# Attention with a K/V cache: the loads at the start are reordered, and the first block's Q projection is interleaved with attention

## The chip, the cores and the metric

The kernel runs on one core of a Trainium2 chip. The metric is device time in microseconds (us); lower is better. A ratio is the mean time of one kernel's fast runs over that of the other's fast runs in the same rounds, so it is not quite the ratio of the medians that are quoted beside it. The engines: PE does the matmuls (PEld loads their weights), ACT the exponentials, DVE the other elementwise work, POOL is the one that gpsimd calls address; SP only issues loads. A DMA queue is named after the engine that issues into it. The DMA share adds up the packets' own times over 16 DMA engines, so it can pass 1.

## The reference

```python
B, Sq, D = 8, 208, 1024
H, Sk, Dh = 32, 1024, 128
# x: (B,Sq,D); k_cache, v_cache: (B,H,Sk,Dh); wq: (D,H*Dh); wo: (H*Dh,D); all bfloat16

def reference(x, k_cache, v_cache, wq, wo):
    q = transpose((x @ wq).reshape(B, Sq, H, Dh), 0, 2, 1, 3)
    scores = einsum("bhqd,bhkd->bhqk", q, k_cache) * (Dh ** -0.5)
    p = softmax(scores, axis=-1)
    o = einsum("bhqk,bhkd->bhqd", p, v_cache)
    return transpose(o, 0, 2, 1, 3).reshape(B, Sq, H * Dh) @ wo
```

## The kernel before

The work is cut into 32 blocks (4 groups of 8 heads, times 8 batches) of 8 units; a unit is one head of one batch. Units are pipelined: PE makes the scores of the next unit while ACT takes the exponential, and PE multiplies by V one half unit later. Two lists of small pieces fill PE's gaps: one piece of Q projection for a later block, and one piece of output projection, per unit. K and x come in by DMA transpose on the SP queue, V by plain copy on the SP queue, and the weights by plain copy on the gpsimd queue.

```python
    xT = const.tile([128, DT, NTOK], BF16, name="xT_all")
    nc.sync.dma_start_transpose(out=xT[:], in_=xf)          # all 8 batches of x, 3.4 MB
    # ... cut ...
    def load_wq_half(g, half):
        w = w_pool.tile([128, DT, HH * 128], BF16, name=f"wq_g{half}")
        c0 = (g * hg + half * HH) * 128
        nc.gpsimd.dma_start(out=w[:], in_=wq[:, c0:c0 + HH * 128].rearrange("(t p) n -> p t n", p=128))
        wq_tiles[(g, half)] = w

    def load_wo(g):
        wo_g = w_pool.tile([128, hg, N], BF16, name="wo_g")
        nc.gpsimd.dma_start(out=wo_g[:], in_=wo[g * hg * 128:(g + 1) * hg * 128, :].rearrange("(h p) n -> p h n", p=128))
        wo_tiles[g] = wo_g

    def load_kv(g, b):
        kts, vs = [], []
        for ck in range(NCKK):                              # once: all 8 heads, 2 MB
            h0 = g * hg + ck * hck
            kT_c = kt_pool.tile([128, hck * Sk], BF16, name="kT_c")
            nc.sync.dma_start_transpose(out=kT_c[:], in_=k_cache[b, h0:h0 + hck].rearrange("h s d -> (h s) d"))
            kts.append(kT_c)
        for ck in range(NCKV):                              # twice: 4 heads, 1 MB each
            h0 = g * hg + ck * hcv
            v_c = v_pool.tile([128, hcv, T, Dh], BF16, name="v_c")
            nc.sync.dma_start(out=v_c[:], in_=v_cache[b, h0:h0 + hcv].rearrange("h (p t) d -> p h t d", t=T))
            vs.append(v_c)
        # ... cut ...
    def start_qproj(bi):
        # ... cut: makes the 8 pieces of block bi ...
        if bi == 0:
            load_wq_half(g2, 0)
            load_wq_half(g2, 1)
        if bi + 1 < NB and blocks[bi + 1][0] != g2:         # a weight-group change: load the next wq
            g3 = blocks[bi + 1][0]
            pa, pb = pieces[HH - 1], pieces[hg - 1]
            pieces[HH - 1] = lambda: (pa(), load_wq_half(g3, 0))
            pieces[hg - 1] = lambda: (pb(), load_wq_half(g3, 1))
        qfill.add(pieces)

    load_wo(0)
    start_qproj(0)
    kv_of[0] = load_kv(*blocks[0])
    qfill.drain()                                           # all Q of block 0
    if NB > 1:
        start_qproj(1)
        qfill.run(1)
    # ... cut: scores of unit 0; then for every unit: scores of the next, PV, sums, norm ...
        qfill.run(1)
        # ... cut: one piece of output projection ...
```

## Time and profile before

| | before |
|---|---|
| time, median of 4 runs (range) | 846.31 us (844.71 to 849.56) |
| span of the profiled run | 846.7 us |
| first matmul | 34.70 us |
| first score matmul | 42.11 us |
| K of block 1 landed (issue plus time to landing) | 41.2 + 16.3 = 57.5 us |

The page of the kernel before: the busy time of the engines, then the span in 40 slices of 21 us, in tenths of busy time.

```profile
PE 772.1 (91%) x7181; PEld 655.6 (77%) x7233; DVE 622.4 (74%) x1889; ACT 590.7 (70%) x1281; POOL 10.9 (1%) x16
...
PE   0299999999999999999999999999999999999983
...
DMA  9999877658979767567997957867888987976500
```

PE is full from the third slice to the end of the body, so a microsecond saved at the start, before PE is full, should reach the end. The DMA engines are over 90% busy in each of the first four slices.

The timeline of the kernel before, first 45 us (start, duration, engine, line, operation, output and input, count; in brackets the idle time of the engine before it and what ended it):

```profile
0.74 31.27 SPq L197 DMA_TRANSPOSE xT_all<-in_x_dram  x1
1.26 1.02 POOL L232 DMA_DIRECT2D wo_g<-in_wo_dram  x1 [0.81 <-POOLq L553]
2.27 1.76 POOL L227 DMA_DIRECT2D wq_g<-in_wq_dram  x2
...
32.07 7.94 SPq L240 DMA_TRANSPOSE kT_c<-in_k_cache_dram  x1
34.70 2.93 PE L262 MATMUL q<-xT_all,wq_g 128*128 128x208 bf16 x16 [34.70 <-DMA xT_all<-in_x_dram]
...
41.23 14.19 SPq L240 DMA_TRANSPOSE kT_c<-in_k_cache_dram  x1
42.11 0.74 PEld L307 LDWEIGHTS <-kT_c 128*128 128x128 bf16 x8 [0.16 <-DMA kT_c<-in_k_cache_dram]
```

PE waits 34.7 us for the transposed x, then gets K of block 0 at 42.1 us. The SP queue is held by each transpose while it is being issued, so the loads behind it wait. From its first matmul PE needs 28.5 us to the first score of unit 8 (the first unit of block 1), with one more wait for a load, of 1.24 us for V; K of block 1 has landed 5.7 us before it is used. So before the change the gate is x, and not yet K of block 1. From the view of PE alone (no wait stands behind the line):

```profile
63.22 0.88 PE L307 MATMUL s_ps<-qT_gb,kT_c 128*128 128x208 bf16 x8
```

The windows of the kernel before (window, its length, busy time and count of each engine, granted clock, DMA share, GB/s):

```profile
2.00:10.00 8.00, 0.00 (x0) 0.00 (x0) 0.00 (x0) 0.03 (x1) 2.03 (x3) 1.00 1.08 233
10.00:18.00 8.00, 0.00 (x0) 0.00 (x0) 0.00 (x0) 0.00 (x0) 0.00 (x0) 1.00 1.04 362
18.00:26.00 8.00, 0.00 (x0) 0.11 (x1) 0.00 (x0) 0.00 (x0) 0.00 (x0) 1.00 1.31 98
26.00:34.00 8.00, 0.00 (x0) 0.00 (x0) 0.00 (x0) 0.00 (x0) 0.00 (x0) 1.00 1.22 267
```

The third row: the DMA engines count as fully busy (1.31) and move only 98 GB/s. The DMA view of the second and the third window says who was served (q1 is the SP queue with the transposes, q0 the gpsimd queue with the weights; packets, MB, share of 16 engines):

```profile
q0 software_dynamic: 686, 2.67, 87.9%
q1 hardware_dynamic: 866, 0.22, 15.7%
...
q1 hardware_dynamic: 1100, 0.28, 115.7%
q0 software_dynamic: 136, 0.50, 15.8%
```

### The profile page before, as it was taken

The numbers are of one execution on the slowest core, as the hardware profiler recorded it, in microseconds if no ns is written. First come the engines' busy times: TensorE is split into PE (matmuls) and PEld (weight loads), VectorE is DVE, ScalarE is ACT, GpSimd is POOL, SyncE is SP. The second block draws the span as 40 slices with busy tenths as digits, with TensorE's granted clock in tenths as the row PEclk, the third lists the DMA queues.
The fourth block names the chain that finished last, engine by engine and source line by source line (L and its number), as shares of the span: only waits on it lengthen the run. The fifth ranks groups of instructions, "written<-read, shape, count | busy, mean of one in ns | idle before, by whom it ended". The sixth has DMA issues, their size and how long they took to land.

```text
span 846.7 us, 18458 instructions
## 1 busy us (share of the span) xinstructions
PE 772.1 (91%) x7181; PEld 655.6 (77%) x7233; DVE 622.4 (74%) x1889; ACT 590.7 (70%) x1281; POOL 10.9 (1%) x16
## 2 busy tenths in 40 slices
PE   0299999999999999999999999999999999999983
PEld 0288888888788888878788888888888888888861
DVE  0077777777777778777777777777777888888893
ACT  0087687777668778767767868677876868777770
POOL 1000000000000000000000000000000000000000
PEclk9999999999999999999999999999999999999998
DMA  9999877658979767567997957867888987976500
GB/s 248 214 297 198 179 170 200 152 152 221 225 166 283 200 138 191 145 176 204 186 258 208 214 139 188 198 152 199 185 233 215 229 203 184 212 167 179 155 26 29
DMA packets 318433, 159.07 MB, mean 188 GB/s; under 512 B 278146, under 2 KB 281474, under 8 KB 318338
## 3 DMA queue, kind: packets, MB, share of 16 engines
q1 hardware_dynamic: 314050, 141.04, 70.9%
q0 software_dynamic: 4288, 16.78, 6.8%
q8 instruction: 58, 0.95, 0.5%
q14 instruction: 37, 0.30, 0.1%
HBM read 83.89 MB, written 3.41 MB: 103 GB/s over the span
## 4 chain that ended last, share of the span: by engine, by line
issue 46%; PE 28%; DVE 13%; ACT 7%; DMA 4%; POOL 1%; DVEq 0%; POOLq 0%
PE po L278 11%; DVE t L329 7%; ACT pT L310 7%; PE o_ps L320 6%; PE q L262 5%; PE s_ps L307 4%; DMA wq_g<-in_wq_dram 4%; DVE oT L350 2%; DVE qT_gb L216 2%; DVE t1c L333 1%; PE o_ps L339 0%; ACT rinv L343 0%; DVE o_sb L293 0%; POOL wq_g L227 0%; DVE oT L352 0%
## 5 line engine op out<-in xcount | busy, mean ns | idle before, releaser
L310 ACT ACTIVATE pT<-s_ps 128x832 bf16<-128x832 f32 x512 | 414.2, 860 | 226.2 <-PE s_ps L307 224.1
L262 PE MATMUL q<-xT_all,wq_g 128*128 128x208 bf16 x2048 | 249.3, 253 | 41.3 <-DMA xT_all<-in_x_dram 34.7
L320 PE MATMUL o_ps<-pT,v_c 128*128 128x208 bf16 x2048 | 241.0, 252 | 16.0 <-DVE oT L350 7.9
L307 PE MATMUL s_ps<-qT_gb,kT_c 128*128 128x208 bf16 x2048 | 241.7, 253 | 0.0
L262 PEld LDWEIGHTS <-wq_g 128*128 128x128 bf16 x2048 | 187.4, 98 | 49.2 <-DMA wq_g<-in_wq_dram 24.5
L307 PEld LDWEIGHTS <-kT_c 128*128 128x128 bf16 x2048 | 207.8, 144 | 19.6 <-issue 0.3
L320 PEld LDWEIGHTS <-v_c 128*128 128x128 bf16 x2048 | 182.7, 97 | 32.9 <-issue 25.0
L278 PE MATMUL po<-wo_g,oT 128*128 128x512 bf16 x780 | 190.3, 379 | 6.0 <-DVE o_sb L293 2.3
L329 DVE TENSOR_TENSOR t<-pT 128x832 bf16<-128x832 bf16 x256 | 151.5, 592 | 41.4 <-ACT pT L310 29.4
L329 DVE TENSOR_TENSOR t<-t 128x416 bf16<-128x416 bf16 (+1 forms) x512 | 161.3, 315 | 8.8
L333 DVE TENSOR_SCALAR_CACHE_REDUCE t1c<-t 128x208 bf16<-128x208 bf16 x256 | 94.6, 370 | 87.0 <-PE o_ps L339 64.7
L278 PEld LDWEIGHTS <-oT 128*128 128x128 bf16 x832 | 80.4, 98 | 77.7 <-issue 3.2
L216 DVE CAST qT_gb<-q 128x416 bf16<-128x416 f32 x128 | 75.1, 587 | 41.3 <-PE q L262 40.5
L343 ACT ACTIVATE rinv<-lnrs 128x208 f32<-128x208 f32 x256 | 97.1, 379 | 8.0
L341 ACT ACTIVATE lnrs<-o_ps 128x208 f32<-128x208 f32 x256 | 89.6, 350 | 0.9 <-PE o_ps L339 0.9
L350 DVE TENSOR_TENSOR oT<-o_ps,rinv 128x208 bf16<-128x208 f32 (+10 forms) x256 | 83.4, 326 | 0.9 <-ACT rinv L343 0.8
L339 PE MATMUL o_ps<-t1c,ones_bf 128*128 128x208 bf16 x256 | 64.7, 253 | 0.1
L290 DVE TENSOR_TENSOR acc<-po,acc 128x512 f32<-128x512 f32 x52 | 36.0, 692 | 16.8 <-PE po L278 16.8
L343 ACT ACTIVATION_READ_ACCUMULATOR rinv<-lnrs 128x1 f32 x256 | 47.9, 187 | 0.0
L293 DVE TENSOR_TENSOR o_sb<-po,acc 128x512 bf16<-128x512 f32 x26 | 18.0, 691 | 10.2 <-PE po L278 10.2
L339 PEld LDWEIGHTS <-ones_bf 128*128 128x128 bf16 x256 | 25.0, 98 | 0.0
L216 DVE COPY acc<-po 128x512 f32<-128x512 f32 x26 | 18.0, 692 | 8.3 <-PE po L278 8.3
(27 smaller groups left out, 76.3 us busy)
## 6 DMA issues: line engine op xcount, KB each, us to landing
v_c<-in_v_cache_dram SPq DMA_DIRECT2D x64, 1024.0 KB, 5.6
wo_g<-in_wo_dram POOLq DMA_DIRECT2D x4, 2048.0 KB, 10.1
wq_g<-in_wq_dram POOLq DMA_DIRECT2D x8, 1024.0 KB, 13.6
out_dram<-o_sb SPq DMA_DIRECT2D x26, 128.0 KB, 2.0
kT_c<-in_k_cache_dram SPq DMA_TRANSPOSE x32, 11.7
xT_all<-in_x_dram SPq DMA_TRANSPOSE x1, 33.9
flag_d<-bad_i SPq DMA_DIRECT2D x1, 0.0 KB
```

The lines of the kernel that those rows point to most:

```text
L216: nc.vector.tensor_copy(out=out_ap, in_=in_ap)
L262: nc.tensor.matmul(q2[:, j, :Sq], lhsT=wq_h[:, t, hw * 128:(hw + 1) * 128], rhs=xT[:, t, b * Sq:(b + 1) * Sq], start=(t == 0), stop=(t == ...
L278: nc.tensor.matmul(po[:rows, :CW], lhsT=oT[:, hl, r0:r0 + rows], rhs=wo_g[:, hl, c * CW:(c + 1) * CW], start=(hl == 0), stop=(hl == hg - 1))
L307: nc.tensor.matmul(s_ps[:, jj // npb, (jj % npb) * Sq:(jj % npb + 1) * Sq], lhsT=kv[:, t, :], rhs=qT_gb[:, hl, :], start=True, stop=True)
L310: nc.scalar.activation(out=pT[:, half * T2:(half + 1) * T2, :].rearrange("p (a b) s -> p a (b s)", a=2), in_=s_ps[:, :, :npb * Sq], func=A ...
L320: nc.tensor.matmul(o_ps[:, :Sq], lhsT=v_c[:, hh, t, :], rhs=pT[:, t, :], start=(t == 0), stop=(t == T - 1))
L329: nc.vector.tensor_tensor(out=nxt[:], in0=cur[:, :n2, :], in1=cur[:, n2:n, :], op=ALU.add)
L333: nc.vector.tensor_scalar(out=t1c[:], in0=cur, scalar1=T1_CLAMP, scalar2=None, op0=ALU.min, op1=ALU.max, accum_out=chk_hi[:, u["idx"]:u["i ...
L339: nc.tensor.matmul(o_ps[:, 256:256 + Sq], lhsT=ones_bf[:], rhs=u["t1"][:, 0, :], start=True, stop=True)
L341: nc.scalar.activation(out=lnrs[:], in_=o_ps[:, 256:256 + Sq], func=ACT.Ln)
L343: nc.scalar.activation(out=rinv[:], in_=lnrs[:], func=ACT.Exp, scale=-1.0, accum_out=chk[:, u["idx"]:u["idx"] + 1])
L350: nc.vector.tensor_tensor(out=oT[:, u["hl"], c0:c0 + n1], in0=u["o_ps"][:, :n1], in1=u["rinv"][:, :n1], op=ALU.mult)
```

## The change

The intent: start PE earlier. Only what the first units need is loaded first (208 rows of x, the first half of wq, two K heads, the first V half); half of block 0's Q pieces run before the first unit and the rest beside it, two per unit. Q pieces are doubled also at each weight-group change, so that the next wq loads are issued earlier.

```diff
     xT = const.tile([128, DT, NTOK], BF16, name="xT_all")
-    nc.sync.dma_start_transpose(out=xT[:], in_=xf)
@@ load_kv
-    def load_kv(g, b):
+    def load_kv(g, b, first=False):
             kT_c = kt_pool.tile([128, hck * Sk], BF16, name="kT_c")
-            nc.sync.dma_start_transpose(out=kT_c[:], in_=k_cache[b, h0:h0 + hck].rearrange("h s d -> (h s) d"))
+            if first and ck == 0 and hck > 2:
+                nc.sync.dma_start_transpose(out=kT_c[:, :2 * Sk], in_=k_cache[b, h0:h0 + 2].rearrange("h s d -> (h s) d"))
+            else:
+                nc.sync.dma_start_transpose(out=kT_c[:], in_=k_cache[b, h0:h0 + hck].rearrange("h s d -> (h s) d"))
@@ after each V half
             vs.append(v_c)
+            if first and ck == 0:
+                load_wq_half(g, 1)
+                load_wo(g)
+                if hck > 2:
+                    nc.sync.dma_start_transpose(out=kts[0][:, 2 * Sk:], in_=k_cache[b, g * hg + 2:g * hg + hck].rearrange("h s d -> (h s) d"))
+                if B > 1:
+                    nc.sync.dma_start_transpose(out=xT[:, :, Sq:], in_=xf[Sq:, :])
@@ start_qproj
-        if bi == 0:
-            load_wq_half(g2, 0)
-            load_wq_half(g2, 1)
         if bi + 1 < NB and blocks[bi + 1][0] != g2:
             # ... cut, unchanged ...
+            fast_q[0] = HH
@@ the start
-    load_wo(0)
+    load_wq_half(0, 0)
+    nc.sync.dma_start_transpose(out=xT[:, :, :Sq], in_=xf[:Sq, :])
     start_qproj(0)
-    kv_of[0] = load_kv(*blocks[0])
-    qfill.drain()
+    kv_of[0] = load_kv(*blocks[0], first=True)
+    qfill.run(HH)
     if NB > 1:
         start_qproj(1)
-        qfill.run(1)
+    fast_q[0] = max(fast_q[0], hg + HH)
@@ every unit (an assertion is cut)
-        qfill.run(1)
+        qfill.run(2 if fast_q[0] > 0 else 1)
+        fast_q[0] = max(0, fast_q[0] - 2)
```

More of the change, by code (lines that the diff above doesn't have):

```diff
@@ L393, in mha_fast @@
     ofill = Fifo()
+    fast_q = [0]
     def start_qproj(bi):
@@ L440, in mha_fast @@
                 assert len(qfill) <= (hg if bi + 2 < NB else 0), "Q-proj of the next block must be complete"
+            elif bi == 0 and hg - len(qfill) + (hg if NB > 1 else 0) < nxt["hl"] + 1 + (hg if NB > 1 else 0):
+                need = nxt["hl"] + 1
+                done = (2 * hg if NB > 1 else hg) - len(qfill)
+                assert done >= need, (done, need)
             bind(nxt)
```

## The prediction

> **What bounds the kernel now.** The 40-slice strip shows PE at 9 tenths from slice 3 on at full clock; the windows give PE 19.0 to 19.5 us of every 20. So PE sets the body; only the start and the tail are slack. The timeline has the first matmul at 34.70 us, released by the transposed load of all of x. wq's first half had landed at 23.8. K of block 0 landed at 42.1, its first V half at 46.1, K of block 1 at 57.5. The DMA share is about 0.9 to 1.3 throughout: the start is bound by DMA volume.
>
> **What the change does.** No matmul is added or removed. Comparing the built programs, PE's order differs only in the first ~310 matmuls and in ~245 at each of three weight-group changes. It splits the x load (208 rows first, 1456 after K), splits the first K load (2 heads, then 6), puts wq before wo, and issues the first V half ahead of the other K heads. The same 11.4 MB still cross before block 0 is complete.
>
> **The start, costed.** By 10 us 0.85 MB of transposes and 1.0 MB of weights had moved, so I estimate that batch 0's x, wq's first half and two K heads are in at 10 to 12 us. But from 10 to 26 us the transposes crawled (0.5 MB) while weight loads drained. I expect this again: the other K heads land near 32, the rest of x (3 MB, at the 256 GB/s transposes had alone) near 44. PE works from ~11 to ~20, stalls for K, works to ~43, then waits in order at block 1's first Q projection for the rest of x. Before reached that point of the work (about 155 matmuls) at 53.4, so ~9 us are available. Next, K of block 1 gates unit 8's first score: the bytes ahead of it are unchanged, so it lands near 57.5 again, where before did that score at 63.2. This is tighter: about 6 us net, of the 24 us that the first matmul moves up. The Trainium skill, "DMA: Bandwidth & Descriptors", section "Issuing engines are not separate DMA queues", says that DMAs of different issuers run on the same 16 engines and interleave; the saturated DMA share agrees. So reordering mostly moves waits.
>
> **Group changes.** Two Q pieces per unit for two units put ~1.6 us more PE work (16 matmuls at about 0.1 us pitch) into units that also carry output projection, and leave two units without filler, where ACT (about 2.3 us a unit) holds the pace. The wq wait this could remove is ~0.7 us in all. Estimated loss: ~2 us over three.
>
> **Prediction: 841 us, 80% range 836 to 846.** Chances: faster by over 2% 0.03, within 2% 0.95, slower 0.02.
>
> **What would show it.**
> - First matmul at 9 to 13 us; PE idle in two gaps, released by K (to ~32) and by the rest of x or the second V half (to 44 to 50): together 20 us or more.
> - K of block 1 lands at 55 to 60 and unit 8's first score follows at once; block 2's first score at about 80 instead of 86.2.
> - Body (100 to 780 us) within 2 us, tail unchanged; PE busy still ~772 us.
>
> **What would make it wrong.** If the transposes don't crawl beside weight loads in the new order, the rest of x and K of block 1 land before 40 and 52 us, and the gain reaches 12 us or more. If the second V half (now last) or the rest of x lands after 50, the gain vanishes. The doubled Q pieces may shift it by 2 to 3 us either way.

## The result, and the profile after

| | before | after |
|---|---|---|
| median (range, runs) | 848.62 us (843.95 to 850.57, 15) | 839.32 us (838.26 to 840.23, 10) |
| ratio of fast runs, 95% interval | | 0.9897 (0.9879 to 0.9916) |
| span of the profiled run | 846.7 us | 837.0 us |
| first matmul | 34.70 us | 10.96 us |
| first score matmul | 42.11 us | 21.73 us |
| K of block 1 landed | 57.5 us | 54.9 us |
| first exponential of unit 8 | 63.77 us | 55.58 us |
| first exponential of unit 16 | 86.75 us | 77.73 us |

The kernel is about 9 us faster, 1.0%. The first matmul moved 24 us, so 15 us of that were lost again. Two instruction streams can be compared unit by unit: ACT takes two exponentials per unit, in the same order of units in both kernels, so the lead of one kernel over another at unit n is the difference of the start times of that unit's first exponential in the two traces. The lead is 20.0 us at unit 0, 18.6 at unit 4, 8.2 at unit 8, 9.02 at unit 16, and 8.9 to 9.5 from there to the end, but for dips at the weight-group changes. Of the 15 us that were lost, 3.7 went before unit 0, 1.4 by unit 4, and 10.4 between units 4 and 8 (the lead is still 19.2 at unit 6).

The page of the kernel after:

```profile
PE 776.0 (93%) x7180; PEld 658.2 (79%) x7233; DVE 622.3 (74%) x1889; ACT 590.2 (71%) x1281; POOL 10.9 (1%) x16
...
PE   2689999999999999999999999999999999999983
...
DMA  9999578778779687558969957768868986876500
```

The timeline of the kernel after, first 56 us:

```profile
1.26 1.90 POOL L226 DMA_DIRECT2D wq_g<-in_wq_dram  x2 [0.81 <-POOLq L568]
...
10.96 2.96 PE L271 MATMUL q<-xT_all,wq_g 128*128 128x208 bf16 x16 [10.96 <-DMA wq_g<-in_wq_dram]
...
21.73 1.61 PE L316 MATMUL s_ps<-qT_gb,kT_c 128*128 128x208 bf16 x8 [5.39 <-DMA kT_c<-in_k_cache_dram]
...
29.92 0.58 PE L316 MATMUL s_ps<-qT_gb,kT_c 128*128 128x208 bf16 x4 [2.76 <-DMA kT_c<-in_k_cache_dram]
...
41.91 2.63 PE L271 MATMUL q<-xT_all,wq_g 128*128 128x208 bf16 x16 [2.76 <-DMA xT_all<-in_x_dram]
...
54.96 0.58 PE L316 MATMUL s_ps<-qT_gb,kT_c 128*128 128x208 bf16 x4 [1.50 <-DMA kT_c<-in_k_cache_dram]
```

One wait of 34.7 us has become five: wq at 10.96, two K heads at 21.73, the other K heads at 29.92, the rest of x at 41.91, K of block 1 at 54.96. The last one sets the time of all that follows, but only by 1.50 us: from 41.91 on PE works without a gap until it waits for K, so with K alone earlier unit 8 could have started no sooner than 53.5. The two loads that gate this stretch stand in one queue, the rest of x ahead of K of block 1. The chain of waits of the kernel after, followed back from 70 us (start, duration, what), shows it as one line of loads on the SP queue:

```profile
2.22 12.56 SPq L240
14.83 0.58 SPq L247
15.47 12.11 SPq L253
27.62 12.09 SPq L255
39.76 0.58 SPq L247
40.38 14.53 DMA kT_c<-in_k_cache_dram
54.96 0.58 PE s_ps L316 x4
```

The same windows of the kernel after (the third is split where the slow stretch ends):

```profile
2.00:10.00 8.00, 0.00 (x0) 0.00 (x0) 0.00 (x0) 0.03 (x1) 2.02 (x3) 1.00 1.05 225
10.00:18.00 8.00, 4.70 (x32) 3.87 (x32) 1.18 (x2) 0.00 (x0) 0.00 (x0) 1.00 1.00 361
18.00:20.00 2.00, 0.00 (x0) 0.00 (x0) 0.00 (x0) 0.00 (x0) 0.00 (x0) 0.59 1.20 168
20.00:26.00 6.00, 4.27 (x29) 3.95 (x30) 1.56 (x5) 2.51 (x4) 0.00 (x0) 0.57 1.15 305
```

The slow stretch of before is short here: the last weight packet starts at 20.3 us instead of 26.0. In its place there is a new thing, a granted clock of about 0.6 after PE had been idle. The Trainium skill, "TensorE: Matmul & The Clock Gate", section "What's actually happening", says that the PE clock falls to half after an idle window of about 3.4 us and comes back after about 3.4 us of work. The return agrees with this trace, the fall only roughly: the recorded grant is 0.5 from 18.4 to 25.2 us and from 42.3 to 45.7 us, so it came back 3.5 us after work had resumed at 21.73, but fell 2.0 us after PE had gone idle at 16.34, and the second time after a wait of 2.76 us that was already over. The five recorded changes lie 3.41, 6.83, 17.07 and 3.41 us apart, which is 1, 2, 5 and 1 times 3.41 us. With it, 8 score matmuls took 1.61 us at 21.73 where 0.88 us is usual, and PE's busy time rose by 3.9 us. The last slow stretch cost nothing at the end: PE still had 1.50 us to wait for K after it. The 1.00 that the windows print before the first record (14.95 us here, 38.39 in before) is no measurement: the first 16 matmuls took 2.96 and 2.93 us, where 1.59 is usual, so the first work ran slow in both kernels.

### The profile page after: what moved, and what is told of

Its sections match the earlier page's. It is cut to its first block, busy times and chain, and to the rows that moved or that the text cites. A ratio compares the mean times of both kernels' runs of the same rounds, so it can differ in the third digit from the quotient of the medians.

```text
span 837.0 us, 18460 instructions
## 1 busy us (share of the span) xinstructions
PE 776.0 (93%) x7180; PEld 658.2 (79%) x7233; DVE 622.3 (74%) x1889; ACT 590.2 (71%) x1281; POOL 10.9 (1%) x16
## 3 DMA queue, kind: packets, MB, share of 16 engines
HBM read 83.89 MB, written 3.41 MB: 104 GB/s over the span
## 4 chain that ended last, share of the span: by engine, by line
PE 53%; DVE 22%; ACT 14%; SPq 5%; issue 3%; DMA 2%; DVEq 0%
PE po L287 21%; ACT pT L319 13%; DVE t L338 13%; PE o_ps L329 12%; PE q L271 11%; PE s_ps L316 9%; DVE qT_gb L215 3%; DVE oT L359 3%; DVE t1c L342 2%; DMA kT_c<-in_k_cache_dram 2%; SPq L240 2%; SPq L253 1%; SPq L255 1%; PE o_ps L348 1%; ACT rinv L352 1%
## 5 line engine op out<-in xcount | busy, mean ns | idle before, releaser
L271 PE MATMUL q<-xT_all,wq_g 128*128 128x208 bf16 x2048 | 247.1, 255 | 19.2 <-DMA wq_g<-in_wq_dram 11.0
L316 PE MATMUL s_ps<-qT_gb,kT_c 128*128 128x208 bf16 x2048 | 245.1, 254 | 9.9 <-DMA kT_c<-in_k_cache_dram 9.7
L316 PEld LDWEIGHTS <-kT_c 128*128 128x128 bf16 x2048 | 209.6, 144 | 30.7 <-DMA kT_c<-in_k_cache_dram 10.4
L287 PEld LDWEIGHTS <-oT 128*128 128x128 bf16 x832 | 80.4, 98 | 77.2 <-issue 3.2
## 6 DMA issues: line engine op xcount, KB each, us to landing
wo_g<-in_wo_dram POOLq DMA_DIRECT2D x4, 2048.0 KB, 10.4
```

The costliest lines, as they stand in the source:

```text
L271: nc.tensor.matmul(q2[:, j, :Sq], lhsT=wq_h[:, t, hw * 128:(hw + 1) * 128], rhs=xT[:, t, b * Sq:(b + 1) * Sq], start=(t == 0), stop=(t == ...
L287: nc.tensor.matmul(po[:rows, :CW], lhsT=oT[:, hl, r0:r0 + rows], rhs=wo_g[:, hl, c * CW:(c + 1) * CW], start=(hl == 0), stop=(hl == hg - 1))
L316: nc.tensor.matmul(s_ps[:, jj // npb, (jj % npb) * Sq:(jj % npb + 1) * Sq], lhsT=kv[:, t, :], rhs=qT_gb[:, hl, :], start=True, stop=True)
```

## The experiments

Theory: the start of the changed kernel is bound by the landing of what stands ahead of K of block 1 in the DMA queues, and part of that time is lost because weights on a second queue crowd out the transposes. Rivals: the earlier first matmul itself pays; the overlap of Q projection with attention pays; the doubled Q pieces at the group changes pay or cost. Medians are us; the lead is against the profile of before. The runs of before on the same chips had medians of 850.47, 850.08 and 850.05 in the three sets (e1 to e6; e7 to e11; e12, e14, e3). All kernels gave correct results.

| label | first matmul | first score | K of block 1 landed | unit 8, first exp. | lead at unit 16 | median | ratio to before |
|---|---|---|---|---|---|---|---|
| before | 34.70 | 42.11 | 57.5 | 63.77 | 0 | (above) | 1 |
| after | 10.96 | 21.73 | 54.9 | 55.58 | 9.02 | 839.32 | 0.9897 |
| e1_no_group_double | 9.98 | 21.32 | 54.3 | 55.17 | 8.52 | 840.53 | 0.9890 |
| e4_x_whole | 36.18 | 41.47 | 60.9 | 65.32 | -1.79 | 850.33 | 0.9998 |
| e5_k_whole | 10.63 | 29.87 | 58.5 | 59.24 | 5.35 | 842.70 | 0.9909 |
| e6_weights_behind_x | 25.02 | 35.12 | 50.2 | 55.42 | 8.35 | 839.73 | 0.9877 |
| e7_x_per_batch | 8.68 | 20.94 | 43.6 | 47.30 | 16.23 | 833.34 | 0.9804 |
| e8_wo_late | 9.52 | 18.34 | 51.8 | 52.78 | 9.82 | 836.93 | 0.9841 |
| e10_one_queue_needed_order | 7.87 | 13.17 | 35.7 | 39.59 | 22.59 | 827.01 | 0.9731 |
| e11_after_weights_on_sp | 7.78 | 12.81 | 52.6 | 53.20 | 12.22 | 837.64 | 0.9858 |
| e12_q_drained_first | 9.14 | 24.44 | 56.9 | 57.52 | 6.58 | 840.31 | 0.9893 |
| e14_weights_on_act_queue | 27.31 | 35.41 | 50.6 | 56.72 | 7.03 | 841.61 | 0.9917 |
| e3_wq_before_wo | 35.64 | 43.33 | 58.6 | 65.04 | -1.29 | 850.05 | 1.0013 |

The times of a start are those of one profiled execution (848.52 us of before, 838.82 of after); the medians rest on 4 to 10 runs.

### What part of the change makes the gain

**e1_no_group_double** (on the kernel after):

```diff
-            fast_q[0] = HH
```

> The changed kernel without the doubled Q pieces at the three weight-group changes; the start is untouched. Theory (the gain is made before unit 16 alone; at the group changes the lead dips by 1.3 us and comes back): same as the changed kernel, 839 us, within 0.7 us, and the lead over before is flat at about 9.0 us from unit 16 on, without dips. My prediction's own term (doubling costs 2 us): 837. Rival (fetching wq earlier is part of the gain): 841 or more.

Measured: 840.53, ratio 0.9890 (0.9868 to 0.9912) against 0.9897 of the change; in the profile the lead is 8.52 at unit 16 and shows no dips, while the kernel after falls by 1.3 us at each group change (9.06 at unit 48, 7.82 at unit 52, 9.06 at unit 60) and has it back some 8 units later. My term of 2 us (837) was wrong. The median alone does not refute the rival: 840.53 lies outside the theory's 0.7 us and just short of the rival's 841. The traces do: from unit 16 to the last unit the lead grows by 0.56 us without the doubled pieces and by 0.43 with them, and the 0.5 us between the two leads is there at unit 16 already. So the doubled pieces cost and pay nothing in these traces: what the doubled units take, the units left without a piece give back.

**e12_q_drained_first** (on the kernel after; the assertion that goes with the overlap is left out):

```diff
-    qfill.run(HH)
+    qfill.drain()
-    fast_q[0] = max(fast_q[0], hg + HH)
+    fast_q[0] = max(fast_q[0], 2)
```

> The changed kernel with its load order, but with the program's overlap of Q projection and attention undone: all 8 Q pieces of block 0 stand ahead of the first unit, and only one unit doubles its pieces of block 1. Theory (the load order alone makes the gain; K of block 1 near 55 us decides): within 1.5 us of the changed kernel, gain over before 8 to 10 us. Rival (the overlap is a part of the gain): gain 5 us or less.

Measured: 840.31, ratio 0.9893 (0.9853 to 0.9934). The runs give the whole gain without the overlap in the program's text; the profiled execution was a slower one of them, with K of block 1 at 56.9. One caution: the built program interleaves by a scheduler of its own, and even here two Q pairs of block 0 stand between scores of the first units. So this shows that asking for the overlap is not needed, not that PE overlaps nothing.

**e4_x_whole** (on the kernel after):

```diff
-    nc.sync.dma_start_transpose(out=xT[:, :, :Sq], in_=xf[:Sq, :])
+    nc.sync.dma_start_transpose(out=xT[:], in_=xf)
-                if B > 1:
-                    nc.sync.dma_start_transpose(out=xT[:, :, Sq:], in_=xf[Sq:, :])
```

> The changed kernel with all of x loaded in one transpose at the head of the queue; wq before wo, the K split, V early and the overlap of Q with attention stay. Theory (the queue is bound by volume and PE needs 30 us of work between first matmul and unit 8): the first matmul goes back to about 33 us, K of block 1 still lands at 54 to 58, but PE then reaches unit 8 only at about 63: nearly all of the gain is lost, 846 to 849. Rival (overlapping Q with attention saves PE time of its own): at most half is lost, 843 or less.

Measured: 850.33, ratio 0.9998: nothing is left. The first matmul is back at 36.18 us and PE needs its 29 us from there to unit 8. The K landing, 60.9, was later than expected.

**e3_wq_before_wo** (on the kernel before):

```diff
-    load_wo(0)
     start_qproj(0)
+    load_wo(0)
```

> The kernel before with wq issued ahead of wo on gpsimd, nothing else. Theory (x gates the first matmul, weights are early enough): wq lands about 10 us earlier, x still at 33 to 36, the kernel within 1.5 us of before. Rival (wq's place is part of the gain): 3 us or more faster.

Measured: 850.05, ratio 1.0013 (0.9972 to 1.0054), with x landing at 35.6. The order of the weights alone does nothing. With e4 this leaves the split of x as the step without which the rest is worth nothing.

**e5_k_whole** (on the kernel after): the load of two heads and the later load of six become one.

```diff
-            if first and ck == 0 and hck > 2:
-                nc.sync.dma_start_transpose(out=kT_c[:, :2 * Sk], in_=k_cache[b, h0:h0 + 2]...)
-            else:
+            if True:
                 nc.sync.dma_start_transpose(out=kT_c[:], in_=k_cache[b, h0:h0 + hck]...)
-                if hck > 2:
-                    nc.sync.dma_start_transpose(out=kts[0][:, 2 * Sk:], in_=k_cache[b, g * hg + 2:g * hg + hck]...)
```

> The changed kernel with the first K load whole (8 heads ahead of the first V half) instead of 2 heads and 6. Theory (only the landing of K of block 1 near 55 us matters, what comes before has slack): the first score moves from 21.7 to about 29 us, yet unit 8 starts within 1.5 us of where it did and the kernel is 839 to 841. Rival (early first scores are what pays): loses most of those 7 us, 845 or more.

Measured: 842.70, ratio 0.9909 (0.9887 to 0.9930). The first score came 8.1 us later (29.87), the kernel lost 1.0 us by the ratios, whose intervals overlap, 3.4 by the medians and 3.7 by the lead at unit 16: between the theory and the rival, nearer the theory. Unit 8 moved 3.7 us in the profile, not the 1.5 at most that was expected, because K of block 1 itself landed later, at 58.5: all 2 MB of K now stood beside the weights (25.6 us of issue on the SP queue). So the landing of K of block 1 is not a constant of the bytes; the order shifts it. The next runs are about that.

### What the second queue costs

**e6_weights_behind_x** (on the kernel before; the same edit in the loads of wq and wo):

```diff
-        nc.gpsimd.dma_start(out=w[:], ...)
+        (nc.sync if g == 0 else nc.gpsimd).dma_start(out=w[:], ...)
```

> The kernel before with one thing changed: the first weight loads (wo, then both wq halves) are issued from SP behind x, in one queue, instead of beside it from gpsimd. Same bytes, same order of the rest, no overlap. Theory (DMA engines alternate packet by packet between queues, one 256-byte transpose packet for each 4 KB weight packet, and transposes wait for the engine that still has weight packets; that wastes some 8 us between 18 and 26 us): x lands at about 14 to 16 us, wq at about 27, K of block 0 at about 33 instead of 42, and the kernel gains 7 to 9 us, about 840. Rival (volume alone counts; bytes move at one total rate in any arrangement): K of block 0 still lands at 41 to 43 and the kernel is at 847 to 849.

Measured: 839.73, ratio 0.9877 (0.9852 to 0.9902). Without any change of the work's order this gains as much as the whole change. The windows of e6, and after them the line of its timeline with the first matmul:

```profile
2.00:10.00 8.00, 0.00 (x0) 0.00 (x0) 0.00 (x0) 0.03 (x1) 0.00 (x0) 1.00 1.20 270
10.00:18.00 8.00, 0.00 (x0) 0.00 (x0) 0.00 (x0) 0.00 (x0) 0.00 (x0) 1.00 1.10 282
18.00:26.00 8.00, 0.98 (x6) 0.87 (x7) 0.00 (x0) 0.00 (x0) 0.00 (x0) 1.00 1.07 387
```

```profile
25.02 2.96 PE L262 MATMUL q<-xT_all,wq_g 128*128 128x208 bf16 x16 [25.02 <-DMA wq_g<-in_wq_dram]
```

The transposes run alone at 290 GB/s (581 KB in every 2 us of the packet records; the first two windows also hold the start and the switch), then the weights at 387; there is no slow stretch. x landed at 15.0 us, and K of block 0 at 35.1 (33 was expected), 7 us earlier than in before. The rival, that bytes move at one rate however they are arranged, falls.

**e14_weights_on_act_queue** (on the kernel before): as e6, with `nc.scalar` in place of `nc.sync`, so that the weights are again beside x, in a second queue of hardware.

> The kernel before with one thing changed: the first weight loads go out from ACT, beside x in a second hardware queue, instead of from gpsimd. In the one-queue run the weight packets were 1 to 2 KB, not 4 KB, so packet-by-packet sharing gives the transposes two to four times the bytes. Theory A (sharing between any two queues costs by packet size): x lands at 24 to 29 us, between the one-queue 15 and the 34.7 of before, and the slow stretch (under 100 GB/s) is gone or under 3 us; K of block 0 at 34 to 38; gain 4 to 8 us. Theory B (any second queue starves transposes and leaves a slow tail, whoever issues): x at 33 or later, gain under 2 us.

Measured: 841.61, ratio 0.9917 (0.9876 to 0.9958), x at 27.2: theory A. The DMA view of e14 from 10 to 16 us (q10 is the ACT queue with wq, q1 the transposes), and then its windows:

```profile
q10 hardware_dynamic: 1710, 1.73, 81.5%
q1 hardware_dynamic: 1709, 0.44, 32.1%
```

```profile
10.00:16.00 6.00, 0.00 (x0) 0.10 (x1) 0.00 (x0) 0.00 (x0) 0.00 (x0) 1.00 1.14 362
16.00:26.00 10.00, 0.00 (x0) 0.00 (x0) 0.00 (x0) 0.00 (x0) 0.00 (x0) 1.00 1.26 294
```

1710 packets against 1709: the engines serve the two queues packet for packet. With wq packets of 1 KB the transposes get a quarter of the weights' bytes, with the 4 KB packets of gpsimd a twelfth to a sixteenth. The Trainium skill, "DMA: Bandwidth & Descriptors", section "Queues, rings and completion order", says that each DMA engine round-robins between the queue rows at packet granularity; these counts agree. When the ACT queue is empty, the transposes go on at once at 294 GB/s. So sharing by itself only moves bytes from one load to another (362 GB/s in all). Most of the loss of before was the slow stretch from 18 to 26 us: at 98 instead of 290 GB/s it cost 5.3 us by my estimate, of the 7.4 by which x came earlier here. It goes with the gpsimd queue's last packets and is absent with two hardware queues. Whether the queue or its packet size (4 KB against 1 to 2 KB) makes it, no run separates. Note also what the gain was here: the first matmul came 7.4 us earlier and the lead is 7.0, since x and not K of block 1 was the gate.

**e11_after_weights_on_sp** (on the kernel after; edit as in e6):

> The changed kernel with one thing changed: its first weight loads go out on SP, in the same order, instead of on gpsimd. Theory (packet-by-packet sharing with weights is what wastes time): K of block 1 lands at about 45 instead of 54.9, unit 8 starts at 46 to 48, gain over before 15 to 17 us, so that the gain of the one-queue change (8 to 9 us, measured on the kernel before) nearly adds to that of the reordering. Rival (both remove the same loss): no more than 10 us.

Measured: 837.64, ratio 0.9858 (0.9840 to 0.9875): about 12 us, between the theory (15 to 17) and its rival (10 at most). The two gains add only in part. K of block 1 landed at 52.6, not 45; part of that the trace shows. At 24.8 and 49.2 us one packet of 16 KB of another queue (q8, kind "instruction") passes. In the microsecond before it 1130 transpose packets started, in the 2.2 us from its start only 796 and 766. By my estimate 1.5 us of transposes were lost each time, 3 of the 7.6 us. That the packet is the cause is inferred from the coincidence, and the rest stays open.

### What the bytes ahead of K of block 1 cost

**e7_x_per_batch** (on the kernel after):

```diff
+    def load_x(b):
+        nc.sync.dma_start_transpose(out=xT[:, :, b * Sq:(b + 1) * Sq], in_=xf[b * Sq:(b + 1) * Sq, :])
             kts.append(kT_c)
+        if g == 0 and not first and b + 1 < B:
+            load_x(b + 1)
-                if B > 1:
-                    nc.sync.dma_start_transpose(out=xT[:, :, Sq:], in_=xf[Sq:, :])
+                load_x(1)
```

> The changed kernel with x loaded batch by batch: only the 208 rows of batch 1 stand ahead of K of block 1, each later batch's rows follow the K load of the block before. Weights stay on gpsimd. Theory (the start is bound by the bytes that stand ahead of K of block 1): 2.5 MB less stand there, K of block 1 lands near 42 to 45 instead of 54.9, PE work becomes the limit, unit 8 starts at 50 to 52 and the gain over before grows from 9 to about 12 us. Rival (the gain is fixed by the first matmul's time, 11 us in both): no difference from the changed kernel.

Measured: 833.34, ratio 0.9804 (0.9786 to 0.9823), nearly 17 us and more than expected. The first matmul and the first score are at most 2.3 us from those of the kernel after, yet 16.2 us of lead remain at unit 16 instead of 9.0. K of block 1 landed at 43.6, as predicted; PE reached unit 8 at 47.3, before the 50 to 52 that I gave it. From its timelines of SP and of PE, the issue of K of block 1 and the first score of unit 8, which waits for nothing:

```profile
29.04 12.45 SPq L245 DMA_TRANSPOSE kT_c<-in_k_cache_dram  x1
...
46.56 0.52 PE L320 MATMUL s_ps<-qT_gb,kT_c 128*128 128x208 bf16 x4
```

This is the clearest proof of what bound the kernel after: the rest of x in the queue ahead of K of block 1, not the time of the first matmul. It takes away two waits at once: that for x itself, which block 1's Q projection needs (batch 1's rows land at 31.0 instead of 41.9), and that for K of block 1. In the trace of the kernel after, K alone could give back no more than 1.5 us, and x alone nothing, as K would still come at 54.9. No run moves one of the two alone.

**e8_wo_late** (on the kernel after): wo is taken from the start and put on SP behind the first V half of block 1.

```diff
-        nc.gpsimd.dma_start(out=wo_g[:], ...)
+        (nc.sync if g == 0 else nc.gpsimd).dma_start(out=wo_g[:], ...)
             vs.append(v_c)
+            if g == 0 and b == 1 and ck == 0:
+                load_wo(0)
             # ... cut, unchanged ...
-                load_wo(g)
```

> The changed kernel with the first wo load (2 MB) taken off gpsimd and put behind K and the first V half of block 1 on SP. The first matmul does not move (it waits for wq). Theory (weights on the other queue slow the transposes as long as they last): the other six K heads land near 23 instead of 30, the rest of x near 36 instead of 42, K of block 1 near 43 instead of 55, unit 8 starts at 46 to 49, gain over before 14 to 17 us. Rival (first matmul decides): as the changed kernel, 9 us.

Measured: 836.93, ratio 0.9841 (0.9823 to 0.9858), about 13.5 us where 14 to 17 were expected. The profile, of the slowest of its four runs, shows a K landing of 51.8 and a lead of 9.8 only. The direction is right, the size was overestimated: 2 MB of wq on gpsimd still left a slow stretch (12 to 18 us), and there were two slower spells later, near 31 and 49 us, that no weights explain. Each begins with one 16 KB packet of the instruction queue, at 31.3 and at 48.1 us (see e11).

**e10_one_queue_needed_order**: e7 and e8 together, and the first wq halves on SP too.

> The two edits before together, and the first wq halves on SP too, so that one queue carries the start in the order of need. By volume at the 290 GB/s (transposes) and 385 GB/s (weights) that one queue showed, K of block 1 lands near 32 and PE becomes the limit: about 255 matmuls at 0.1 us after a first matmul at 7 to 8, plus cold-clock and dependency losses, so unit 8 starts at 39 to 42 and the gain over before is 21 to 24 us, which is over 2 per cent. Rival (some other cost of the start, say the Q evictions or the clock, holds it): under 14 us.

Measured: 827.01 (826.09 to 827.67), ratio 0.9731 (0.9714 to 0.9748): 23 us, as expected, and faster than both kernels. From its page, and then from its timeline:

```profile
PE 773.4 (94%) x7181; PEld 655.7 (80%) x7233; DVE 622.0 (75%) x1889; ACT 590.6 (72%) x1281; POOL 8.3 (1%) x13
...
PE   5899999999999999999999999999999999999983
```

```profile
7.87 2.93 PE L276 MATMUL q<-xT_all,wq_g 128*128 128x208 bf16 x16 [7.87 <-DMA xT_all<-in_x_dram]
...
22.77 10.74 SPq L245 DMA_TRANSPOSE kT_c<-in_k_cache_dram  x1
```

K of block 1 lands at 22.77 + 12.9 = 35.7 us (near 32 was expected), 3.9 us before unit 8's first exponential: K of block 1 is no longer the limit, PE is; it still waited 2.90 us for the other K heads of block 0, at 23.4.

## Why the prediction was right or wrong

- **Total.** 841 with a range of 836 to 846 was forecast; 839.32 was measured. Against the 846.31 it started from, it forecast a gain of about 5 us; about 9 were made. That the total was only 1.7 us off is in part luck: the gain was 4 us too small, and before was 2.3 us slower in the rounds of the result (848.62) than in the runs that the forecast started from.
- **The mechanism at the start was right.** The first matmul at 10.96 (9 to 13 forecast); unit 8's first score at 54.96, at once when K of block 1 had landed; most of the 24 us lost to new waits. Both gates that it named, the rest of x and then K of block 1, are in the trace; it put K about 3 us behind x as a limit, and it was 1.5. e7 and e10 show that the loads ahead of K of block 1 were the limit.
- **Mis-sized: the landings.** "It lands near 57.5 again" was 54.9, and 55 to 60 was given as the test. The other K heads (32 forecast, 29.9), the rest of x (44, 41.9) and K of block 1 are all 2 to 3 us early. I had carried the slow stretch of 18 to 26 us over unchanged; in the new order it ended with the last gpsimd packet at 20.3 (23.5 in e12, where K of block 1 came at 56.9); why it ended sooner is not shown. With it, block 2's first score came at 77.2 instead of 80. "the bytes ahead of it are unchanged, so it lands near 57.5 again" is the step that was off, by 2.6 us: e5, e6 and e14 moved this landing between 50.2 and 58.5 with the same bytes ahead.
- **Wrong: the group changes.** "Estimated loss: ~2 us over three" was nothing. The leads dip by 1.3 us and recover, and e1 without the doubling is not faster. So the units left without a piece gave the time back, where I had thought that ACT would hold them.
- **Wrong: the idle time of PE.** I forecast two gaps of 20 us or more together. After the first Q pieces there were four longer waits for loads of 5.4, 2.8, 2.8 and 1.5 us, 12.4 together.
- **Missed: the clock.** PE busy was forecast at 772 and was 776.0. The half-clock stretches after idle hold 6.9 us of work, of which half, 3.4 us, is extra by my estimate. They did not reach the end of the kernel.
- **Right: the rest.** In the body, 100 to 780 us, PE was busy 662.6 us against 662.3, and the lead changed by less than 0.5 us from unit 16 to the last unit, the dips at the group changes apart.

What stays open: why the gpsimd queue's last packets slow the transposes sevenfold. From 24 to 26 us only 11 weight packets of 164 ns were left, just enough to fill one engine, while all transpose packets took about 190 ns; that would fit transposes that move in step over all engines, but the trace has no engine number and no run tests it. The spells in e8 and e11 fit it too: there a single packet of 16 KB, which took about 1.1 us, goes with a near stop of the transposes. Open is also what else slowed the single queue of e11.

## What to carry to other kernels

When a kernel's start is full of DMA, moving the first matmul says little by itself: find the loads whose landing gates steady work (here x for the *second* block's Q projection, and its K), and take out of their way every byte that is needed later. Within two queues that gave 17 us here (e7), where the change gave 9. Be wary of bulky weights on the gpsimd queue beside small-packet transposes that are needed sooner; with them in the one queue too, in the order of need, the gain was 23 us. On a second hardware queue they cost less (e14). And test an estimate of a landing by the rate at which each queue was served, not by the bytes alone.

## What the Trainium skill lacked or had wrong

- "DMA: Bandwidth & Descriptors", section "Issuing engines are not separate DMA queues", says that issuing from several engines only saves the sequencer's time to initiate. Here the choice of the issuer changed the kernel's time with the same bytes: weights beside x from gpsimd 850.05 us, from ACT 841.61 in the same rounds. The packets differ with it, 4 KB from gpsimd and 1 to 2 KB from ACT.
- The same page, section "Queues, rings and completion order", gives packet round-robin but not its consequence: with 4096-byte weight packets against 256-byte transpose packets, 2.67 MB against 0.22 MB moved in 8 us.
- No page has the slow stretch at the end of a gpsimd load beside transposes: 98 GB/s at a DMA share of 1.31 for 8 us, 135 ns per transpose packet instead of 18. It was 8 us long in before, 2 us in the kernel after, and absent with two hardware queues.
- No page says what one 16 KB packet of the instruction queue costs the transposes beside it: in e11 796 and 766 transpose packets started in 2.2 us, where 1130 started in the microsecond before.
- The same page, section "Latency and other measured facts", gives a DMA transpose 261 GB/s, and 350 to 400 where the source is contiguous. Transposes that had the engines alone ran at 290 GB/s here, for K (contiguous 256-byte rows) and for x alike.
